# Attention stage of an attention-and-experts kernel: second buffers for K, Q and V as loaded, and an order of work taken from a written table of times

## The chip, the cores and the metric

The kernel runs on one core of one Trainium2 chip. The metric is the device time of one execution in microseconds (us). A core has five instruction streams that run side by side and wait for each other by semaphores: TensorE (PE, with its weight loads shown apart as PEld), VectorE (DVE), ScalarE (ACT), GpSimd (POOL) and SyncE (SP), which here issues nearly all DMA transfers of the attention stage. Each stream runs in the order in which the program was written.

## The reference

Attention over 8 batches and 8 heads with 1152 keys of 64 elements, the queries averaged in pairs (576 per head), and then a layer of 8 experts with a fixed capacity:

```python
def _attn_ref(q, k, v):
    B, H, S, D = q.shape                       # 8, 8, 1152, 64, float32
    scale = 1.0 / np.sqrt(D)
    q_pool = q.reshape(B, H, S // 2, 2, D).mean(axis=3)
    scores = scale * np.matmul(q_pool, k.transpose(0, 1, 3, 2))
    scores = scores - np.max(scores, axis=-1, keepdims=True)
    attn = np.exp(scores)
    attn = attn / (np.sum(attn, axis=-1, keepdims=True) + 1e-09)
    return np.matmul(attn, v).astype(np.float32)

def reference(...):
    x = attn_out.transpose(0, 2, 1, 3).reshape(B * S, H * D)   # 4608 x 512
    return _moe_ref(x=x, ...)   # logits x @ w_gate, capacity 576 per expert,
                                # relu(x @ w1[e]) @ w2[e], float32
```

## The kernel before

The work on attention runs over 32 pairs of heads, two heads side by side on the 128 partitions. A pair goes through these steps, named here by the tags of the code:

- Loads on SP: `lq` (queries, tile QD, 576 KB), `lk` (keys, tile KD, in two halves of 288 KB), `lv` (values, tile VD, 576 KB). There is one buffer of each.
- Preparation: `qs` on DVE adds the two queries of each average; `ka` and `qa` on ACT sum absolute values; `ks` (four tiny DVE steps) makes a scale; `qh`, `kh` on ACT and `ql`, `kl` on DVE split Q and K into a high and a low float16 part. `kl` is the last reader of KD. Copies on SP spread the parts over the operand tiles: `s1`, `s2`, `s3` for keys, `s4`, `s5`, `s6` for queries, `bd` for a block-diagonal query operand. `vabs`, `vs`, `vh`, `vl` do the same for V.
- Row maxima: `mm` on PE multiplies high parts into the PSUM tiles mt, `mr` on DVE reduces them (tile MX), `fold`, `augt`, `aug`, `augd` turn them into an extra row of the query operand.
- The main loop of 18 steps a pair: `qk` on PE (two matmuls, tile sc, three PSUM banks in turn), `exp` on ACT (tile P), `pm` on POOL or DVE (tile PM, the rounding rest of P), `av` on PE in groups of one or two steps; `rc` and `x` on DVE divide the result into tile X.
- Every second pair, `gt`, `gc`, `gm`, `gl` apply the gate weights to the finished columns and `store` writes X to DRAM.
- Constant tables for the experts stage (`routing_tables`), and at the start matmuls on constants (`wu`, `wv`) and `fill`s.

All of these are given to `Order.add` with a program position t, an engine, an assumed duration, the resources read and written, and a tag. `Order.emit` derives what must follow what, and then plays a list schedule: it keeps a clock per engine, takes whichever ready step can start first, breaks ties by t plus a hand-found lead per tag (`LEAD`), adds assumed latencies (`OWN`, `WAIT`, `LATE`), and keeps DVE and POOL steps marked `lock` from overlapping in its own clocks. The order in which this play starts the steps is the order in which the instructions are written to the engines. The experts stage has an `Order` of its own.

Of the kernel before, what the change touches and what calls it, by code (L numbers as in the profile page):

```python
# [1433 lines left out]
```

## Time and profile before

| | us |
|---|---|
| median of 3 runs | 1302.24 (1299.56 to 1303.64) |
| the profiled execution, its own time | 1307.96 |
| its span, first to last instruction | 1306.20 |
| PE, DVE, ACT, POOL busy in the span | 1247.8, 1038.2, 769.9, 777.7 |
| attention, first instruction to the last `av` | 802.4 |

Busy time is the union of an engine's instructions. PE's ends are modelled, so a busy PE is not a PE at its peak. The profiled execution took 5.7 us more than the median run; sums over the trace are made against 1307.96.

### The profile page before, as it was taken

The numbers are of one execution on the slowest core, as the hardware profiler recorded it, in microseconds if no ns is written. First come the engines' busy times: TensorE is split into PE (matmuls) and PEld (weight loads), VectorE is DVE, ScalarE is ACT, GpSimd is POOL, SyncE is SP. The second block draws the span as 40 slices with busy tenths as digits, with TensorE's granted clock in tenths as the row PEclk, the third lists the DMA queues.
The fourth block names the chain that finished last, engine by engine and source line by source line (L and its number), as shares of the span: only waits on it lengthen the run. The fifth ranks groups of instructions, "written<-read, shape, count | busy, mean of one in ns | idle before, by whom it ended". The sixth has DMA issues, their size and how long they took to land.

```text
span 1306.2 us, 39238 instructions
## 1 busy us (share of the span) xinstructions
PE 1247.8 (96%) x15419; PEld 1008.1 (77%) x15419; DVE 1038.2 (79%) x2606; ACT 769.9 (59%) x1901; POOL 777.7 (60%) x746
## 2 busy tenths in 40 slices
PE   7899999999999999999999997799999999999996
PEld 4577787777777777777777776587978889798895
DVE  8999999999999999899999985898876767752120
ACT  4588777877877877877877864143333324334330
POOL 5275576565656656656657563257667667586631
PEclk8799999999999999999999998999999999999998
DMA  4655555654654654654655520225445343454301
GB/s 150 154 167 144 156 151 139 174 148 126 186 145 121 178 147 117 177 150 119 181 149 140 126 60 20 66 102 197 170 133 150 130 126 124 151 172 143 125 14 37
DMA packets 123541, 175.25 MB, mean 134 GB/s; under 512 B 49500, under 2 KB 86364, under 8 KB 121180
## 3 DMA queue, kind: packets, MB, share of 16 engines
q1 hardware_dynamic: 114876, 120.29, 34.2%
q0 software_dynamic: 8336, 52.44, 11.5%
q8 instruction: 121, 1.98, 0.7%
q14 instruction: 64, 0.52, 0.1%
q10 hardware_dynamic: 144, 0.02, 0.0%
HBM read 99.63 MB, written 18.87 MB: 91 GB/s over the span
## 4 chain that ended last, share of the span: by engine, by line
PE 72%; DVE 16%; issue 5%; DMA 4%; ACT 1%; SPq 1%; POOL 0%; POOLq 0%; DVEq 0%; ACTq 0%
PE ph L1327 16%; PE av L617 14%; PE po L1357 13%; PE mt L497 8%; PE sc L600 8%; PE sc L601 7%; DVE MX L524 4%; DVE PM L607 4%; DMA KA<-KL 2%; DMA KD<-in_kt_dram 1%; PE mt L658 1%; PE po L1354 1%; DVE KL L442 1%; DMA QA<-QH 1%; PE rt L1001 1%
## 5 line engine op out<-in xcount | busy, mean ns | idle before, releaser
L607 POOL TENSOR_TENSOR PM<-P 128x576 f16<-128x576 f32 x413 | 473.4, 1174 | 312.4 <-ACT P L604 263.8
L604 ACT ACTIVATE P<-sc 128x288 f32<-128x288 f32 x1152 | 396.1, 413 | 162.7 <-PE sc L601 151.4
L524 DVE TENSOR_REDUCE MX<-mt 128x2 f32<-128x768 f32 (+1 forms) x443 | 399.4, 919 | 47.1 <-PE mt L497 43.8
L600 PE MATMUL sc<-QA,KA 128*128 128x288 f16 x1152 | 309.9, 286 | 10.9 <-ACT P L604 8.9
L617 PEld LDWEIGHTS <-P 128*128 128x128 bf16 x5760 | 297.5, 98 | 27.8 <-issue 0.7
L601 PE MATMUL sc<-QB,KB 66*128 66x288 f16 (+1 forms) x1152 | 311.7, 288 | 0.6 <-DMA QB<-AU 0.4
L617 PE MATMUL av<-V,P 128*128 128x65 f16 (+1 forms) x5760 | 306.0, 193 | 1.2 <-DVE V L483 1.2
L617 PE MATMUL av<-V,PM 128*128 128x65 f16 x2880 | 296.4, 195 | 0.0
L617 PEld LDWEIGHTS <-PM 128*128 128x128 f16 x2880 | 265.4, 97 | 1.3 <-issue 1.3
L497 PE MATMUL mt<-KH,BD 128*128 128x384 f16 x837 | 200.2, 326 | 3.4 <-DVE MX L524 1.6
L1357 PE MATMUL po<-W2H,HX 128*128 128x512 f32 x512 | 168.2, 399 | 0.0
L601 PEld LDWEIGHTS <-KB 66*128 66x128 f16 (+1 forms) x1152 | 112.0, 97 | 66.7 <-issue 29.6
L1327 PE MATMUL ph<-XH,W1H 128*128 128x320 f32 (+1 forms) x512 | 153.0, 299 | 1.0 <-issue 0.5
L1327 PE MATMUL ph<-XL,W1H 128*128 128x320 f32 (+1 forms) x512 | 152.4, 298 | 1.6 <-DVE XL L1226 1.5
L1327 PE MATMUL ph<-XH,W1L 128*128 128x320 f32 (+1 forms) x512 | 152.3, 298 | 1.0 <-issue 1.0
L600 PEld LDWEIGHTS <-KA 128*128 128x128 f16 x1152 | 112.9, 98 | 49.5 <-issue 15.7
L1332 ACT ACTIVATE HX<-ph 128x256 fp32r<-128x256 f32 (+1 forms) x128 | 51.5, 413 | 134.0 <-PE ph L1327 125.5
L607 DVE TENSOR_TENSOR PM<-P 128x576 f16<-128x576 f32 x163 | 123.5, 767 | 6.4 <-ACT P L604 5.5
L1357 PE MATMUL po<-W2L,HX 128*128 128x512 f32 (+1 forms) x320 | 127.6, 399 | 0.0
L1336 DVE SCALAR_TENSOR_TENSOR HX<-ph,HX 128x256 fp32r<-128x256 f32 x128 | 52.9, 415 | 81.1 <-ACT HX L1332 77.6
L1357 PEld LDWEIGHTS po<-W2H,HX 128*128 128x128 f32 x512 | 95.3, 189 | 18.5 <-issue 1.7
L497 PEld LDWEIGHTS <-BD 128*128 128x128 f16 x837 | 75.3, 98 | 30.8 <-issue 10.4
(233 smaller groups left out, 1899.7 us busy)
## 6 DMA issues: line engine op xcount, KB each, us to landing
QD<-in_qt_dram SPq DMA_DIRECT2D x32, 576.0 KB
KD<-in_kt_dram SPq DMA_DIRECT2D x64, 288.0 KB
VD<-in_v_dram SPq DMA_DIRECT2D x32, 576.0 KB
QA<-QH SPq DMA_DIRECT2D x128, 72.0 KB
KA<-KH SPq DMA_DIRECT2D x64, 144.0 KB
KB<-KH SPq DMA_DIRECT2D x64, 144.0 KB
KA<-KL SPq DMA_DIRECT2D x64, 144.0 KB
x_dram<-X SPq DMA_DIRECT2D x16, 576.0 KB
```

The source lines that it names most:

```text
L442: od.add(t + 5 + 2 * z, "DVE", 727, lock=1, fn=lambda h=h: nc.vector.scalar_tensor_tensor(KL[0][:, h], KD[0][:, h], sk, KH[i][:, h], op0=O ...
L497: nc.tensor.matmul(out, BD[i][:, j], KH[i][:, ks], start=True, stop=True)
L524: od.add(t, "DVE", d, lambda: nc.vector.tensor_reduce(dst, src, axis=AX.X, op=OP.max), r=[mk], w=[("MX", i, j, c) for j, c in what], tag=" ...
L600: nc.tensor.matmul(c[:, :288], KA[i][:, s, ks], QA[i][:, s, qs], start=True, stop=False)
L601: nc.tensor.matmul(c[:, :288], KB[i][:kr, s, ks], QB[i][:kr, s, qs], start=False, stop=True)
L604: od.add(g + 0.1 + 0.01 * t, "ACT", 293, lambda c=c, qs=qs: nc.scalar.activation(p[:, qs], c[:, :288], AF.Exp, scale=1.0 / UNIT), r=[ck], ...
L607: od.add(g + 0.2, en, dur, lock=1, fn=lambda: eng.tensor_tensor(pm, p, hi, op=OP.subtract), r=[("P32", g % NP, 0), ("P32", g % NP, 1)], w= ...
L617: nc.tensor.matmul(out, w[:, qs], v, start=kb == 0 and j == 0 and y == 0, stop=kb == NKB - 1 and y == 2, skip_group_check=True)
L1327: nc.tensor.matmul(p, a[:, d, fs], b[:, d, qs], start=z == 0, stop=z == 11)
L1332: nc.scalar.activation(HH[:, f, qs], p, AF.Relu)
L1336: V.scalar_tensor_tensor(HL[:, f, 64 + 256 * hf:320 + 256 * hf], p[:, :256], 0.0, h[:, :256], op0=OP.max, op1=OP.subtract)
L1357: nc.tensor.matmul(o[:n], a[:, z, q0:q0 + n], b[:, z], start=z == 0 and y == 0, stop=z == 7, skip_group_check=True)
```

## The change

Tiles KD, QD and VD get a second buffer (pair n uses buffer n % 2), so the load of pair n+1 no longer has to follow the last reader of pair n. The list schedule of the attention stage is replaced by `Timed`: each step has a name (its tag, its index k, and a letter that counts repeats within a pair), and an entry in a table of times in ns. The entry counts from the start of its pair, and pair n starts at n x 23600. Pairs 0 to 3 and the last two (`y`, `z`) have rows of their own; all others use the rows `e` (even) and `o` (odd), so the order repeats every two pairs. `emit` writes, among the steps whose predecessors have been written, the one with the smallest time. Clocks, latencies, leads and the `lock` marks play no part any more. Which engine does which step, durations, tiles other than the three, and the experts stage are unchanged.

```diff
-    od = Order(LEAD, LATE)
-    od.stick = AT["stick"]
+    od = Timed(TIME, PERIOD, npair)
...
-    KD = several(1, [128, S], F32, "KD")
-    QD = several(1, [128, 2, M], F32, "QD")
-    VD = several(1, [128, 2, NKB, D], F32, "VD")
+    KD = several(2, [128, S], F32, "KD")
+    QD = several(2, [128, 2, M], F32, "QD")
+    VD = several(2, [128, 2, NKB, D], F32, "VD")
...
-            od.add(t, "SP", 1200, lambda h=h: nc.sync.dma_start(KD[0][:, h], kt[n][:, h]), w=[("KD", z)],
+            od.add(t, "SP", 1200, lambda h=h: nc.sync.dma_start(KD[n % 2][:, h], kt[n][:, h]), w=[("KD", n % 2, z)],
                    late=2000, tag="lk", k=z)
...
+class Timed(Order):
...
+    def when(self, i):
+        n, name, t = self.names[i]
+        if name is None:
+            return -1e6
+        for p in ("0123" + "-" * self.pairs)[n] + ("yz"[n - self.pairs + 2] if n + 2 >= self.pairs else "-") + "eo"[n % 2]:
+            if p + name in self.table:
+                return n * self.period + self.table[p + name]
+        return t / NSTEP * self.period + self.period
+
+    def emit(self):
+        items = sorted(range(len(self.items)), key=lambda i: (self.items[i][0], i))
...
+        heap = [(self.when(items[i]), i) for i in range(n) if not left[i]]
+        heapq.heapify(heap)
+        done = 0
+        while heap:
+            _, i = heapq.heappop(heap)
+            self.items[items[i]][4]()
+            done += 1
+            for j in users[i]:
+                left[j] -= 1
+                if not left[j]:
+                    heapq.heappush(heap, (self.when(items[j]), j))
...
+PERIOD = 23600
...
+        "0filli": -28725, "0fillj": -12920, "0folda": -21352, "0foldb": -7681, "0foldc": -7038, "0foldd": 13293,
+        "0folde": -14699, "0foldf": -7378, "0foldg": -151, "0foldh": -12930, "0iqa": -16700, "0iqb": -12237,
+        "0iqc": -29805, "0iqd": -12930, "0kaa": -62092, "0kab": -2174, "0kh0a": -47325, "0kh1a": -47135,
...
+        "0kse": -10509, "0lk0a": -50752, "0lk1a": -38077, "0lqa": -47701, "0lva": -18899, "0mca": -11093,
...
+        "1ksa": -53738, "1ksb": -50821, "1ksc": -60593, "1ksd": -47555, "1lk0a": -62969, "1lk1a": -63095,
...
+        "2s41a": -19505, "2s50a": -20003, "2s51a": -31364, "2s60a": -34079, "2s61a": -28738, "2tablesa": -6078,
...
+        "2tablesg": -16860, "2tablesh": -12541, "2tablesi": -14357, "2tablesj": 701, "2tablesk": 7222,
...
+        "eaugdb": -29239, "eaugta": -5367, "eav0a10a": 20821, "eav0a12a": 24000, "eav0a14a": 22376,
+        "eav0a16a": 21085, "eav0a17a": 26168, "eav0a1a": 8204, "eav0a3a": 10245, "eav0a5a": 12272,
...
+        "eexpb8a": -6966, "eexpb9a": -3860, "efolda": -14291, "ekaa": -51818, "ekh0a": -38345, "ekh1a": -37948,
...
+        "elk0a": -61297, "elk1a": -62910, "elqa": -61161, "elva": -28886, "emm0a": -28007, "emm10a": -11157,
+        "emm11a": -10503, "emm12a": -7204, "emm13a": -7242, "emm1a": -28007, "emm2a": -28006, "emm3a": -28007,
...
+        "epm8a": -28584, "epm9a": -34115, "eqaa": -48418, "eqha": -47273, "eqka0a": 509, "eqka10a": 11977,
...
+        "eqkb6a": 7807, "eqkb7a": 7808, "eqkb8a": 8004, "eqkb9a": 12284, "eqla": -38350, "eqsa": -51227,
+        "erc0a": -9682, "erc1a": -14578, "erca": -15138, "ercb": -14666, "es10a": -16229, "es11a": -15107,
+        "es20a": -28887, "es21a": -28767, "es30a": -16422, "es31a": -16463, "es40a": -16508, "es41a": -16583,
+        "es50a": -16584, "es51a": -27951, "es60a": -31159, "es61a": -24359, "evabsa": -12829, "evh0a": -1161,
...
+        "oav0a8a": 17942, "obda": -39843, "obdb": -38791, "oexpa0a": 1968, "oexpa10a": -7384, "oexpa11a": -1477,
...
+        "ogcb": 2554, "ogla": -47730, "ogma": 39737, "ogpa": -45501, "ogta": 20686, "ogtb": 34983, "okaa": -55857,
...
+        "oksc": -60791, "oksd": -46190, "olk0a": -75548, "olk1a": -75143, "olqa": -72386, "olva": -37173,
...
+        "oqka0a": 2054, "oqka10a": 12901, "oqka11a": 13075, "oqka12a": 13711, "oqka13a": 16231, "oqka14a": 13651,
...
+        "os40a": -40304, "os41a": -39329, "os50a": -41912, "os51a": -35235, "os60a": -37173, "os61a": -29675,
...
-    for _ in range(AT["wu"]):
-        od.add(-70, "PE", 60, lambda: nc.tensor.matmul(mt[0][:, 0, :128], ones, ones, start=True, stop=True), w=["m0"])
+    for z in range(AT["wu"]):
+        od.add(-70, "PE", 60, lambda: nc.tensor.matmul(mt[0][:, 0, :128], ones, ones, start=True, stop=True), w=["m0"], tag="wu", k=z)
...
-    od.cur = None
+    od.cur, od.pair = None, 2
     C = routing_tables(nc, top, ident, jp, scratch,
-                       lambda eng, dur, fn: od.add(2 * NSTEP, eng, dur, fn, w=["tables"]))
+                       lambda eng, dur, fn: od.add(2 * NSTEP, eng, dur, fn, w=["tables"], tag="tables"))
```

The same renaming by n % 2 is made in every reader of the three tiles (`split`, `values`). In the table 1625 entries stand; those quoted are the ones that the prediction speaks of.

## Rows read from the trace of the kernel before

**Rows 1.** The page's first lines: the span, and each engine's busy us (share of the span) x instructions.

```profile
span 1306.2 us, 39238 instructions
...
PE 1247.8 (96%) x15419; PEld 1008.1 (77%) x15419; DVE 1038.2 (79%) x2606; ACT 769.9 (59%) x1901; POOL 777.7 (60%) x746
```

**Rows 2.** Busy time of each engine in stretches of the attention stage. The columns are the stretch and its length, busy us (and instructions) of PE, PEld, DVE, ACT and POOL, PE's granted clock, the mean busy share of the DMA engines, and GB/s. Each stretch but the last runs from one maximum reduction to the same one two pairs later, as the chain that ended last shows them (the one that ends at 582.82 holds four pairs). Twelve such two-pair stretches lie between 149.33 and 725.11. The last row is the start, up to pair 1's first matmul on sc.

```profile
149.33:196.50 47.17, 47.05 (x763) 37.06 (x760) 44.71 (x84) 37.57 (x96) 29.55 (x27) 1.00 0.57 154
196.50:243.67 47.17, 47.05 (x763) 37.02 (x760) 44.71 (x84) 37.60 (x96) 29.54 (x27) 1.00 0.56 153
243.67:291.97 48.30, 47.26 (x766) 37.24 (x763) 44.85 (x86) 37.62 (x96) 29.67 (x27) 1.00 0.54 146
...
435.64:484.69 49.05, 47.26 (x766) 37.24 (x763) 44.85 (x86) 37.62 (x96) 29.71 (x27) 1.00 0.54 147
484.69:582.82 98.13, 94.45 (x1520) 73.97 (x1517) 89.82 (x167) 75.35 (x192) 59.29 (x53) 1.00 0.55 147
...
677.80:725.11 47.31, 47.14 (x763) 37.02 (x760) 44.73 (x85) 37.62 (x96) 29.47 (x27) 1.00 0.57 153
0.00:64.18 64.18, 49.75 (x527) 34.71 (x528) 56.51 (x131) 33.51 (x76) 26.66 (x41) 0.79 0.54 152
```

**Rows 3.** Who waited for whom in 243.67 to 582.82 us: us in total, times, longest us.

```profile
ACT VJ L406 <- DMA KD<-in_kt_dram: 8.1, 7, 1.8
PE sc L600 <- ACT P L604: 6.2, 7, 1.1
...
PE sc L600 <- DMA VD<-in_v_dram: 1.7, 1, 1.7
```

**Rows 4.** One place of such a wait, 446 to 457 us, in order of time: start, length, engine, line, operation, tiles; in brackets the idle time before it and what ended it. K's release on DVE, the issues on SP, ACT, and PE.

```profile
446.86 1.54 DVE L442 SCALAR_TENSOR_TENSOR KL<-KD,KS,KH 128x576 f16<-128x576 f32 x2
...
449.21 1.73 SPq L392 DMA_DIRECT2D KD<-in_kt_dram  x2
...
450.96 2.15 ACT L604 ACTIVATE P<-sc 128x288 f32<-128x288 f32 x6 [0.16 <-PE sc L601]
454.88 1.16 ACT L406 ACTIVATE VJ<-KD 128x1152 bf16<-128x1152 f32 x1 [1.77 <-DMA KD<-in_kt_dram]
...
456.48 0.28 PE L600 MATMUL sc<-QA,KA 128*128 128x288 f16 x1 [1.68 <-DMA VD<-in_v_dram]
```

**Rows 5.** Loads and copies on SP: duration in ns (min/median/max) of the issuing instructions on SP, first and last start; then the GB/s of 100 to 300 us in 40 slices.

```profile
L392 SPq DMA_DIRECT2D KD<-in_kt_dram x64: 333/522/1456, 1.2 to 722.7; - x64
...
L389 SPq DMA_DIRECT2D QD<-in_qt_dram x32: 328/530/2188, 0.8 to 713.3; - x32
...
L450 SPq DMA_DIRECT2D QA<-QH x128: 463/595/2037, 10.7 to 760.2; - x128
...
L450 SPq DMA_DIRECT2D KA<-KH x64: 482/595/1982, 12.0 to 759.6; - x64
...
GB/s 252 142 84 236 132 77 36 178 279 145 162 172 119 210 121 26 113 257 148 249 148 97 250 109 62 64 170 261 191 209 81 107 221 121 21 113 186 222 208 168
```

**Rows 6.** The start on DVE and SP, in order of time (columns as in rows 4).

```profile
0.76 0.40 SPq L389 DMA_DIRECT2D QD<-in_qt_dram  x1
1.21 0.91 SPq L392 DMA_DIRECT2D KD<-in_kt_dram  x2
2.17 0.43 SPq L396 DMA_DIRECT2D VD<-in_v_dram  x1
...
1.58 0.64 DVE L384 MEMSET P<- 128x64 f32 x10
...
2.55 3.54 DVE L373 TENSOR_SCALAR ndiag<-scratch 128x576 f32<-128x576 int32 x2
6.01 0.74 DVE L401 TENSOR_TENSOR QS<-QD 128x576 f32<-128x576 f32 x1
...
23.54 0.22 DVE L267 TENSOR_SCALAR before<-jp 128x128 bf16<-128x128 int32 x1
...
26.54 1.80 DVE L276 TENSOR_SCALAR nib<-scratch 128x16 f32<-128x16 int32 x2
...
28.99 1.14 DVE L281 TENSOR_SCALAR diag<-scratch 128x64 f16<-128x64 int32 x1
30.16 1.10 DVE L282 TENSOR_TENSOR diag<-diag,scratch 128x64 f16<-128x64 f16 x1
...
31.58 0.95 DVE L524 TENSOR_REDUCE MX<-mt 128x2 f32<-128x768 f32 x1
...
32.57 0.48 DVE L288 CAST slots<-scratch 128x640 f16<-128x640 int32 x1
```

**Rows 7.** Line 607, the step `pm`: its instructions on POOL and on DVE, duration in ns (min/median/max).

```profile
L607 POOL TENSOR_TENSOR PM<-P x413: 1140/1147/1713, 25.0 to 797.9; 128x576 f16<-128x576 f32 x138
...
L607 DVE TENSOR_TENSOR PM<-P x163: 736/748/1689, 35.6 to 798.9; 128x576 f16<-128x576 f32 x163
```

**Rows 8.** The first matmul on sc of pairs 6, 7 and 8, in order of time (columns as in rows 4).

```profile
182.22 0.28 PE L600 MATMUL sc<-QA,KA 128*128 128x288 f16 x1
...
208.24 0.28 PE L600 MATMUL sc<-QA,KA 128*128 128x288 f16 x1
...
229.39 0.28 PE L600 MATMUL sc<-QA,KA 128*128 128x288 f16 x1
```

More of the change, by code (lines that the diff above doesn't have):

```diff
@@ L1 @@
+import heapq
 import math
@@ L158, in emit, with __init__, add @@
             items[i][4]()
+class Timed(Order):
+    def __init__(self, table, period, pairs):
+        Order.__init__(self)
+        self.table, self.period, self.pairs = table, period, pairs
+        self.pair, self.names, self.seen = 0, [], {}
+    def add(self, t, eng, dur, fn, r=(), w=(), late=0, first=0, tag=None, kind=0, lock=None, k=None):
+        Order.add(self, t, eng, dur, fn, r, w, late, first, tag, kind, lock)
+        name = ("pm" if tag in ("pmP", "pmD") else tag or "o") + ("" if k is None else str(k))
+        z = self.seen[self.pair, name] = self.seen.get((self.pair, name), -1) + 1
+        self.names.append((self.pair, name + "abcdefghijklmnopqrstuvwxyz"[z] if z < 26 else None, t))
+    def when(self, i):
[8 more added lines that the diff above has]
+        items = sorted(range(len(self.items)), key=lambda i: (self.items[i][0], i))
+        writer, readers, n = {}, {}, len(items)
+        need = [set() for _ in range(n)]
+        for i, j in enumerate(items):
+            _, _, _, _, _, r, w, _, _ = self.items[j]
+            for k in r:
+                if k in writer:
+                    need[i].add(writer[k])
+                readers.setdefault(k, []).append(i)
+            for k in w:
+                if k in writer:
+                    need[i].add(writer[k])
+                need[i].update(readers.get(k, ()))
+                readers[k] = []
+                writer[k] = i
+            need[i].discard(i)
+        users, left = [[] for _ in range(n)], [len(x) for x in need]
+        for i, x in enumerate(need):
+            for j in x:
+                users[j].append(i)
+        heap = [(self.when(items[i]), i) for i in range(n) if not left[i]]
[9 more added lines that the diff above has]
+                    heapq.heappush(heap, (self.when(items[j]), j))
+        assert done == n
@@ L300, in attention @@
     psum = ctx.enter_context(tc.tile_pool(name="att_psum", bufs=1, space=PSUM))
-    od = Order(LEAD, LATE)
-    od.stick = AT["stick"]
-    od.early = ("qs", "qh", "bd", "kh", "kl", "ql", "mm", "mc", "mr", "fold", "aug", "augt")
+    od = Timed(TIME, PERIOD, npair)
     jp = const.tile([128, 128], I32, name="jp")
@@ L388, in load @@
     def load(n, t):
-        od.add(t, "SP", 2440, lambda: nc.sync.dma_start(QD[0], qt[n]), w=["QD"], late=2000, tag="lq")
+        od.add(t, "SP", 2440, lambda: nc.sync.dma_start(QD[n % 2], qt[n]), w=[("QD", n % 2)], late=2000, tag="lq")
         for z in range(2):
             h = slice(z * M, z * M + M)
-            od.add(t, "SP", 1200, lambda h=h: nc.sync.dma_start(KD[0][:, h], kt[n][:, h]), w=[("KD", z)],
+            od.add(t, "SP", 1200, lambda h=h: nc.sync.dma_start(KD[n % 2][:, h], kt[n][:, h]), w=[("KD", n % 2, z)],
                    late=2000, tag="lk", k=z)
     def load_v(n, t):
-        od.add(t, "SP", 2500, lambda: nc.sync.dma_start(VD[0], v[n]), w=["VD"], late=2500, tag="lv")
+        od.add(t, "SP", 2500, lambda: nc.sync.dma_start(VD[n % 2], v[n]), w=[("VD", n % 2)], late=2500, tag="lv")
     def split(n, t):
         i = n % 2
-        od.add(t, "DVE", 666, lock=1, fn=lambda: nc.vector.tensor_tensor(QS[0], QD[0][:, 0], QD[0][:, 1], op=OP.add),
-               r=["QD"], w=["QS"], tag="qs")
+        od.add(t, "DVE", 666, lock=1, fn=lambda: nc.vector.tensor_tensor(QS[0], QD[n % 2][:, 0], QD[n % 2][:, 1], op=OP.add),
+               r=[("QD", n % 2)], w=["QS"], tag="qs")
         if n:
-            od.add(t + .5, "ACT", 1150, lambda: nc.scalar.activation(VJ, KD[0], AF.Abs, accum_out=KS[i][:, 0:1]),
-                   r=[("KD", 0), ("KD", 1)], w=[("KN", i)], tag="ka")
+            od.add(t + .5, "ACT", 1150, lambda: nc.scalar.activation(VJ, KD[n % 2], AF.Abs, accum_out=KS[i][:, 0:1]),
+                   r=[("KD", n % 2, 0), ("KD", n % 2, 1)], w=[("KN", i)], tag="ka")
         else:
@@ L439, in split @@
             h = slice(z * M, z * M + M)
-            od.add(t + 4 + 2 * z, "ACT", 670, lambda h=h: nc.scalar.activation(KH[i][:, h], KD[0][:, h], AF.Copy, scale=sk),
-                   r=[("KD", z), ("SK", i)], w=[("KH", i, z)], tag="kh", k=z)
+            od.add(t + 4 + 2 * z, "ACT", 670, lambda h=h: nc.scalar.activation(KH[i][:, h], KD[n % 2][:, h], AF.Copy, scale=sk),
+                   r=[("KD", n % 2, z), ("SK", i)], w=[("KH", i, z)], tag="kh", k=z)
             od.add(t + 5 + 2 * z, "DVE", 727, lock=1, fn=lambda h=h: nc.vector.scalar_tensor_tensor(
-                KL[0][:, h], KD[0][:, h], sk, KH[i][:, h], op0=OP.mult, op1=OP.subtract),
-                r=[("KD", z), ("SK", i), ("KH", i, z)], w=[("KL", z)], tag="kl", k=z)
+                KL[0][:, h], KD[n % 2][:, h], sk, KH[i][:, h], op0=OP.mult, op1=OP.subtract),
+                r=[("KD", n % 2, z), ("SK", i), ("KH", i, z)], w=[("KL", z)], tag="kl", k=z)
     def spread(n, t):
@@ L726, in attention @@
     od.cur = None
-    for _ in range(AT["wu"]):
-        od.add(-70, "PE", 60, lambda: nc.tensor.matmul(mt[0][:, 0, :128], ones, ones, start=True, stop=True), w=["m0"])
-    for _ in range(AT["wv"]):
+    for z in range(AT["wu"]):
+        od.add(-70, "PE", 60, lambda: nc.tensor.matmul(mt[0][:, 0, :128], ones, ones, start=True, stop=True), w=["m0"], tag="wu", k=z)
+    for z in range(AT["wv"]):
         od.add(-42, "PE", 54, lambda: nc.tensor.matmul(av[:, :128], ones, ones, start=True, stop=True),
-               r=[("CM", 0, 0)], w=["av"], first=-1)
+               r=[("CM", 0, 0)], w=["av"], tag="wv", k=z)
     for i in range(2):
@@ L736, in attention @@
         base = NSTEP * (n - 1)
-        od.cur = n
+        od.cur = od.pair = n
         if n == 0:
@@ L776, in attention @@
     for g in range(npair * NSTEP):
-        od.cur = g // NSTEP
+        od.cur = od.pair = g // NSTEP
         step(g)
     for n in range(1, npair, 2):
-        od.cur = None
+        od.cur, od.pair = None, n
         g = NSTEP * n + NSTEP
@@ L793, in attention @@
         store(n, g + LAG + 1)
-    od.cur = None
+    od.cur, od.pair = None, 2
     C = routing_tables(nc, top, ident, jp, scratch,
-                       lambda eng, dur, fn: od.add(2 * NSTEP, eng, dur, fn, w=["tables"]))
+                       lambda eng, dur, fn: od.add(2 * NSTEP, eng, dur, fn, w=["tables"], tag="tables"))
     od.emit()
```

30 lines of the change are left out of this document (20 added, 10 removed), and 307 rows, old and new, of tables (LATE, LEAD, TIME).

## The prediction

> **What bounds the kernel now.** I read four things in this order: the engines' shares, the busy time in equal pieces of the attention stage, the list of waits in the worse pieces, and one such wait instruction by instruction. The shares say that PE is busy for 96% of the span [rows 1], so time can only come from PE's few idle places or from work that leaves PE's queue, and the change takes no work away. The reader should then look at the pieces of two pairs each [rows 2]. The program repeats there, and the best pieces take 47.17 us, with PE busy for 47.05 and DVE for 44.71. Two engines are nearly full: DVE has 47.17 - 44.71 = 2.46 us left in two pairs. Other pieces hold the same work (763 or 766 matmuls, 96 ACT instructions) and take 48.30, 49.05, and 98.13 for four pairs, while PE's busy time grows by only 0.2 in a two-pair piece. The difference is idle PE.
>
> The waits name it [rows 3]: in 243.67 to 582.82 us PE waits for ACT's `exp` 7 times, 6.2 us, and once more 1.7 us under the name of a V load; ACT waits for the K load 7 times, 8.1 us. One of them in detail [rows 4]: `kl`, the last reader of the only K buffer, ends at 448.40. SP issues both K halves between 449.21 and 450.94. ACT has finished its `exp`s by 453.11 and comes to `ka`, which needs K: it stands until 454.88, some 4.3 us after the second issue began. The `exp`s behind `ka` are late by as much, the three score banks are full, and PE sits 1.68 us before its next `qk`. The V load in that row is only the event nearest in time; the `qk` waits for a bank. So a K buffer that is freed late, a load of about 4 us and a place on ACT's queue too close to it cost about 1 us in more than half of the middle periods.
>
> **The change, part by part.**
>
> *Second buffers and earlier loads.* The table puts the K load of an even pair 62.9 and 61.3 us ahead of its pair and `ka` at 51.8, thus about 10 us between them; for an odd pair 75.5 and 55.9, about 20. Before, it was 4.3. The release by `kl` no longer matters, since the other buffer's last reader lies a pair back. What it is worth: twelve periods lie between 149.33 and 725.11, which is 575.78 us; twelve undisturbed ones are 12 x 47.17 = 566.04 [rows 2]. That is 9.7 us. I take all of it, because every stall in these pieces has the same shape. Bounds: 0, if `ka` is still late, and 9.7.
>
> *The repeated order.* Its bounds are wide. If every hidden wait went, a period could fall to DVE's 44.71, 13 x 2.46 = 32 us less over pairs 4 to 29; if it hits as badly as the worst piece, 49.05, it loses 13 x 1.88 = 24. I take 0, for the table looks like the undisturbed periods of this trace: an even and the following odd pair start at 182.22 and 208.24, the next even one at 229.39, 26.02 and 21.15 us apart [rows 8], and the table's first `qk` of an even and an odd pair are 23.6 + 2.05 - 0.51 = 25.1 apart, then 22.1. Work per engine is the same. At the places where PE needs DVE at once (`augt` after `fold`, `gt` after a maximum) I find in the table about the distance the trace has.
>
> *SP's queue.* To find a step's place I take the later of its own entry and those of the steps that it must follow. Around 31 us after an even pair's start this bunches transfers: seven operand copies of the next even pair (0.79 MB), four of the next odd one (0.29), then between them the K halves and Q of the pair four ahead (1.15). That is 14 issues, 11 x 0.595 + 3 x 0.525 = 8.1 us by the medians of rows 5, so Q is issued near 30.6 + 8.1 = 38.7 and read by `qs` on DVE at 94.4 - 51.2 = 43.2. Behind it on SP wait only copies needed 10 us and more later. The 2.2 MB take 8.0 us at the best slice's 279 GB/s [rows 5] and 14.6 at the 153 of a mean period [rows 2]: 38.6, or 45.2. I take no cost, since a bunch issued in one go is nearest to a full slice, and keep up to 3 us of DVE wait a period as the upper end (45.2 plus the landing, against 43.2).
>
> The Trainium skill (DMA: Bandwidth & Descriptors, Anatomy of one DMA) gives a transfer about 2.0 us plus its bytes over 436 GB/s, estimated 2.7 us for a K half; rows 4 show 4.3 from issue to use, so the measurement is the slower one. By the page's figures Q would land near 42.1 and nobody would wait, and the sum would be the same as mine.
>
> *The start.* The constant tables leave it: DVE spends 26.54 to 31.58 mostly on them, 5.0 us, and two shorter bits at 23.54 and 32.57 [rows 6]; they go to pairs 2 and 3, where DVE's 2.46 us of slack a period takes half. Against that, the memsets and the two `ndiag` steps, done from 1.58 to 6.09 while DVE waited for Q, get entries at -12.9 and -12.2, among the work ahead of the first `qk`: 1.0 us and up to 3.5. And pair 1's K halves (576 KB) stand on SP ahead of pair 0's second K half (-39.5 against -38.1): 2.1 to 3.8 us by the two rates above, in a start whose first loads were issued from 0.76 on and read from 6.01 on. DVE has 64.18 - 56.51 = 7.7 us idle in the start [rows 2] to soak up some. Bounds: 5 us better to 8 worse; I take 0, as the two sides are of one size. Pairs 30 and 31 and the experts stage: 0, same work.
>
> *Sum.* 1307.96 - 9.7 = 1298.3 for the profiled execution. The median run is 5.7 us faster than that; carried over, 1292.5. Part of the 5.7 may be milder stalls, and then less is to be had, at the least 9.7 - 5.7 = 4. I say **1293**, and 1287 to 1300 for this case alone.
>
> **Rivals.**
>
> *The period shrinks too.* For it: some 2.5 us a period are idle on DVE, and the table moves many steps by a microsecond or two. Against it: two engines at 95% and more, chained through two maximum banks and three score banks. Half of the floor's gain is 16 us: 1277.
>
> *Given back.* `ka` is on time, but another step in the fixed order now stands about 0.7 us a period, for example the even pair's `augt`, placed 1.8 us after the last `mm`, which DVE must first reduce (0.95 each [rows 6]). 13 x 0.75 = 9.7, hence no change: 1302. That the buffers alone do nothing, because `ka` still waits, ends at the same time; 10 us against 4.3 speaks against it.
>
> *Slower: the burst.* If SP's bunch moves at 153 GB/s, Q comes up to 3.5 us late and DVE stands in `qs`, with the reductions behind it. It decides from 2.46 us of wait on, DVE's slack; at 3.5 it is 13 x 1.0 us over the forecast, 1306, and with the start's 5 worse 1311. Against it: five of the forty slices move 250 GB/s or more [rows 5], so the engines can do it when there is work queued.
>
> *Slower: DVE and POOL collide.* The list schedule kept `lock` steps apart in its clocks; the table doesn't know them. A `pm` takes 736 to 1689 ns on DVE and 1140 to 1713 on POOL [rows 7], and tiny table steps stretch to 1.1 us [rows 6]: one collision is about 0.95. Slack covers 2.6 a period; five of the ten DVE `pm`s hit would cost 4.75 - 2.46 = 2.3, so 30 us: 1323. Against it: the order is close to that of before, where the medians are at the minima. The Trainium skill (SBUF — State Buffer, Who interferes with whom) has the pair of ports as an exclusive lock that goes to whoever issues first; the longest rows agree with it.
>
> **Chances.** Forecast 0.53, shorter period 0.11, given back or no effect 0.18, burst 0.12, collisions 0.06. What this measurement can tell from no change is 0.3%, 3.9 us: under 1298.3 counts as faster, over 1306.1 as slower. From the forecast 0.03 falls within: faster 0.61, same 0.21, slower 0.18. The range 1276 to 1309 leaves out the far end of the shorter period, the collisions and the worse half of the burst.
>
> **What would show it.** In the profile after: ACT's wait for the K load gone or under 1 us in all after 150 us; even pieces of 47.2 us throughout, with the same busy times; PE's waits for `exp` near zero there; SP issuing an even pair's K loads about 10 us or more before `ka`. Wrong would be: DVE waiting for the Q load, pieces that all have the same new length other than 47.2, longer `pm` rows, or pair 1 starting more than 5 us away from 64.18.

## The result, and the profile after

The changed kernel is slower: 1310.64 us against 1302.24 in the median, a ratio of 1.0051 (95% interval 1.0030 to 1.0071), where 1293 and "faster" had been predicted. Measured a second time, on another chip, the ratio was 1.0055 (1.0034 to 1.0077). The page of the changed kernel's profiled execution, which took 1306.12 us (4.5 us less than its median run), begins:

```profile
span 1304.3 us, 39111 instructions
...
PE 1239.5 (95%) x15419; PEld 1004.5 (77%) x15419; DVE 1053.9 (81%) x2606; ACT 784.8 (60%) x1901; POOL 783.1 (60%) x746
```

The two spans say nothing here: the profiled execution of before [rows 1] was a long one among its runs, that of after a short one. The stages can be compared. The columns are as in [rows 2]; the cuts are the first matmuls on sc of pairs 1, 2, 3, 4 and 28 and the last `av`; the last row is the experts stage. Before:

```profile
0.00:64.18 64.18, 49.75 (x527) 34.71 (x528) 56.51 (x131) 33.51 (x76) 26.66 (x41) 0.79 0.54 152
64.18:87.46 23.28, 21.65 (x328) 16.51 (x326) 22.30 (x43) 19.26 (x49) 15.73 (x13) 1.00 0.52 143
87.46:113.48 26.02, 25.92 (x424) 20.27 (x421) 24.97 (x50) 21.87 (x54) 14.79 (x13) 1.00 0.65 182
113.48:135.04 21.56, 21.20 (x345) 16.75 (x342) 19.72 (x36) 15.76 (x42) 14.76 (x13) 1.00 0.44 114
135.04:710.82 575.78, 566.13 (x9099) 444.97 (x9096) 537.58 (x1001) 451.34 (x1152) 355.53 (x312) 1.00 0.55 150
710.82:802.38 91.56, 91.37 (x1539) 73.00 (x1536) 74.30 (x133) 65.29 (x173) 59.06 (x55) 1.00 0.32 85
802.38:1306.19 503.81, 471.83 (x3189) 401.92 (x3185) 302.83 (x1220) 162.92 (x355) 291.14 (x299) 0.97 0.37 120
```

After:

```profile
0.00:65.89 65.89, 45.91 (x513) 31.94 (x513) 52.53 (x114) 37.46 (x82) 23.85 (x30) 0.84 0.55 153
65.89:90.44 24.55, 23.78 (x370) 18.54 (x369) 22.32 (x39) 17.80 (x46) 18.50 (x24) 0.95 0.60 151
90.44:120.28 29.84, 25.80 (x390) 19.31 (x388) 27.42 (x69) 21.67 (x52) 15.11 (x13) 1.00 0.41 116
120.28:142.50 22.22, 21.56 (x342) 16.93 (x340) 21.64 (x37) 16.93 (x45) 15.48 (x13) 1.00 0.60 161
142.50:714.35 571.85, 562.01 (x9094) 444.36 (x9093) 549.68 (x1000) 460.39 (x1152) 360.95 (x312) 1.00 0.57 152
714.35:806.06 91.71, 90.48 (x1532) 72.52 (x1529) 77.25 (x131) 65.92 (x171) 58.20 (x55) 1.00 0.30 77
806.06:1304.32 498.26, 469.95 (x3195) 400.86 (x3191) 303.07 (x1221) 164.65 (x355) 291.03 (x299) 0.98 0.37 122
```

Row by row, after minus before: +1.71, +1.27, +3.82, +0.66 (7.46 lost by pair 4), -3.93 in the twelve two-pair periods of pairs 4 to 27, +0.15 in pairs 28 to 31. Attention is 3.68 us longer. The experts stage, the same code, was 5.55 us shorter in this execution; in the second profile of the changed kernel, the run after_again, it took 504.96 us, and attention 806.99. So a gain is there, and the first four pairs lose nearly twice as much. The forecast for attention comes to 802.38 - 9.74 = 792.64 us; of the 13.42 by which it was missed, 7.46 are lost by pair 4, 5.81 in the twelve periods and 0.15 in the last pairs.

The gain first. ACT's wait for K, the first row of [rows 3], is gone. The place that answers to [rows 4], in order of time: SP issues both K halves at 427.60, and `ka` reads them at 445.01, 17.4 us later, without waiting.

```profile
427.60 1.34 SPq L662 DMA_DIRECT2D KD<-in_kt_dram  x2
...
445.01 1.18 ACT L676 ACTIVATE VJ<-KD 128x1152 bf16<-128x1152 f32 x1
```

The best two-pair periods now take 47.45 us, not 47.17 [rows 2], and ten of the twelve are within 0.2 us of that. One of the best (columns as above):

```profile
190.09:237.54 47.45, 46.76 (x758) 36.99 (x757) 45.73 (x84) 38.35 (x96) 30.08 (x26) 1.00 0.56 152
```

PE is idle for 0.69 us of it, against 0.12 before. Two short waits stand in every period, `mm` for a maximum bank and the one-column matmul on V's maxima for ACT's `vabs`; their sums over 135 to 758 us (us, times, longest) and one example of each:

```profile
PE mt L767 <- DVE MX L794: 5.8, 13, 0.5
...
PE mt L739 <- ACT VJ L736: 2.9, 13, 0.2
```

```profile
586.81 0.16 PE L739 MATMUL mt<-VM,ones 128*128 128x1 bf16 x1 [0.22 <-ACT VJ L736]
...
593.89 0.27 PE L840 MATMUL mt<-ident,CM 128*9 128x128 f32 x1
...
594.59 0.65 PE L767 MATMUL mt<-KH,BD 128*128 128x384 f16 x3 [0.42 <-DVE MX L794]
```

The loss is clearest in pair 2 (29.84 against 26.02 us). The larger block of constant tables, 98.39 to 102.20 us, stands there in one piece on DVE; a reduction waits behind it, and PE 1.08 us for that:

```profile
97.53 0.95 DVE L794 TENSOR_REDUCE MX<-mt 128x2 f32<-128x768 f32 x1
98.39 1.62 DVE L548 TENSOR_SCALAR nib<-scratch 128x16 f32<-128x16 int32 x2
...
101.99 0.21 DVE L564 CAST TAB<-scratch 128x1 f16<-128x1 int32 x2
...
102.36 0.95 DVE L794 TENSOR_REDUCE MX<-mt 128x2 f32<-128x768 f32 x1
```

```profile
103.36 0.48 PE L767 MATMUL mt<-KH,BD 128*128 128x384 f16 x2 [1.08 <-DVE MX L794]
```

The waits of PE in pair 2, from 90.44 to 120.28 us, make up nearly all of the 3.8 us (before, pair 2 had none over 0.15):

```profile
PE sc L870 <- ACT P L874: 1.8, 5, 0.7
...
PE mt L767 <- DVE MX L794: 1.3, 2, 1.1
...
PE mt L942 <- DVE VE L743: 0.4, 1, 0.4
...
PE av L887 <- DVE X L909: 0.2, 1, 0.2
```

So the largest part is PE waiting five times for an `exp` to free a score bank. Pair 1's 1.27 us are mostly the clock. From 60.0 to 64.9 us PE was busy for only 2.04 us; from 64.9 to 68.3 it was then granted the lower of its two levels (1.2 and 2.4 GHz). In the kernel before, pair 1 ran at the upper one throughout. At the rate of the rest of the pair, 349 matmuls in 21.37 us, the 23 that fall into pair 1 at the lower level would take 1.4 us and not 2.4, an estimate of 1.0 us lost:

```profile
60.00:64.90 4.90, 2.04 (x16) 0.85 (x13) 4.67 (x15) 2.15 (x5) 0.00 (x0) 1.00 0.07 16
...
65.89:68.30 2.41, 2.41 (x23) 1.85 (x22) 2.26 (x4) 2.08 (x5) 0.67 (x1) 0.50 0.27 61
...
68.30:90.44 22.14, 21.37 (x349) 16.69 (x347) 20.06 (x35) 15.72 (x41) 17.84 (x24) 1.00 0.63 161
```

At the very start the first `qk` comes at 33.90 us, not 23.70, but pair 1 only 1.7 us later than before.

### The profile page after: what moved, and what is told of

It is laid out like the page before. It is cut to its first block, busy times and chain, and to the rows that moved or that the text cites. A ratio compares the mean times of both kernels' runs of the same rounds, so it can differ in the third digit from the quotient of the medians.

```text
span 1304.3 us, 39111 instructions
## 1 busy us (share of the span) xinstructions
PE 1239.5 (95%) x15419; PEld 1004.5 (77%) x15419; DVE 1053.9 (81%) x2606; ACT 784.8 (60%) x1901; POOL 783.1 (60%) x746
## 4 chain that ended last, share of the span: by engine, by line
PE 72%; DVE 16%; issue 5%; DMA 3%; SPq 1%; ACT 1%; POOL 1%; DVEq 0%; POOLq 0%; ACTq 0%
PE ph L1597 16%; PE av L887 14%; PE po L1627 13%; PE mt L767 9%; PE sc L870 8%; PE sc L871 8%; DVE MX L794 5%; DVE PM L877 3%; DMA KA<-KL 2%; DVE KL L712 2%; PE po L1624 1%; PE mt L928 1%; SPq L720 1%; PE rt L1271 1%; DVE QS L671 1%
## 5 line engine op out<-in xcount | busy, mean ns | idle before, releaser
L877 POOL TENSOR_TENSOR PM<-P 128x576 f16<-128x576 f32 x413 | 479.2, 1185 | 310.0 <-ACT P L874 297.9
L874 ACT ACTIVATE P<-sc 128x288 f32<-128x288 f32 x1152 | 403.5, 412 | 136.0 <-PE sc L871 120.8
L794 DVE TENSOR_REDUCE MX<-mt 128x2 f32<-128x768 f32 (+1 forms) x443 | 392.9, 923 | 22.8 <-PE mt L767 16.3
L887 PEld LDWEIGHTS <-P 128*128 128x128 bf16 x5760 | 288.6, 98 | 22.9 <-issue 2.3
L887 PE MATMUL av<-V,P 128*128 128x65 f16 (+1 forms) x5760 | 296.5, 192 | 1.5 <-issue 1.3
L887 PE MATMUL av<-V,PM 128*128 128x65 f16 x2880 | 289.2, 195 | 0.1
L1606 DVE SCALAR_TENSOR_TENSOR HX<-ph,HX 128x256 fp32r<-128x256 f32 x128 | 53.6, 420 | 77.4 <-ACT HX L1602 77.2
L1627 PEld LDWEIGHTS po<-W2H,HX 128*128 128x128 f32 x512 | 95.4, 189 | 16.8
```

What stands on the lines that cost most here:

```text
L794: od.add(t, "DVE", d, lambda: nc.vector.tensor_reduce(dst, src, axis=AX.X, op=OP.max), r=[mk], w=[("MX", i, j, c) for j, c in what], tag=" ...
L874: od.add(g + 0.1 + 0.01 * t, "ACT", 293, lambda c=c, qs=qs: nc.scalar.activation(p[:, qs], c[:, :288], AF.Exp, scale=1.0 / UNIT), r=[ck], ...
L877: od.add(g + 0.2, en, dur, lock=1, fn=lambda: eng.tensor_tensor(pm, p, hi, op=OP.subtract), r=[("P32", g % NP, 0), ("P32", g % NP, 1)], w= ...
L887: nc.tensor.matmul(out, w[:, qs], v, start=kb == 0 and j == 0 and y == 0, stop=kb == NKB - 1 and y == 2, skip_group_check=True)
L1606: V.scalar_tensor_tensor(HL[:, f, 64 + 256 * hf:320 + 256 * hf], p[:, :256], 0.0, h[:, :256], op0=OP.max, op1=OP.subtract)
L1627: nc.tensor.matmul(o[:n], a[:, z, q0:q0 + n], b[:, z], start=z == 0 and y == 0, stop=z == 7, skip_group_check=True)
```

## The experiments

Every ratio is to the kernel before, run on the same chip in the same sitting, with its 95% interval. Several kernels use the old list schedule as a clock: `Timed` also plays it, with one buffer of each as before, writes nothing from it, and keeps each step's start, shifted so that pair 4's first `qk` falls on its time in the table.

**The change once more**, unaltered:

> The changed kernel as it is, beside the other runs of this chip, for its profile and its ratio to the kernel before here. If the ratio of 1.005 is the two orders' doing, it comes again between 1.003 and 1.008, with pair 4 at 142 to 143 us and even pieces of 47.5 us. Attention up to the last av should again be some 4 us longer than in the kernel before (806.1 against 802.4), and what is left of the ratio stands in the experts stage, whose code is the same.

Measured: 1.0055, as given above; pair 4 starts at 144.2 us, and pair 2 took 30.6.

**One part alone.** Second buffers, and every engine's instructions in the order of before:

```diff
-    KD = several(1, [128, S], F32, "KD")
+    KD = several(2, [128, S], F32, "KD")
...
-            od.add(t, "SP", 1200, lambda h=h: nc.sync.dma_start(KD[0][:, h], kt[n][:, h]), w=[("KD", z)],
+            od.add(t, "SP", 1200, lambda h=h: nc.sync.dma_start(KD[n % 2][:, h], kt[n][:, h]), w=[("KD", z)],
```

> The kernel before with a second buffer for K, Q and V; its planner still plans with one, so every engine's instructions stand in the same order as before. If the freeing of the K buffer by kl was what made K late, the waits of ACT for the K load go, the two-pair pieces fall to 47.2 us and the time drops by 5 to 10 us against the kernel before. If the place of the load on SP's queue was what made it late (in the profile of before SP waits for a reader of K, Q or V some 13 us in all over 576 us, at most 1.6 us at a time), the load is issued at most 1 to 1.5 us sooner, a part of ACT's waits stays, and the time falls by 0 to 3 us.

Measured: 1.0016 (0.9993 to 1.0039), no difference. ACT still waits for K 7 times, 6.5 us. The sum, and one place on DVE, SP and ACT: `kl` ends at 447.87, SP issues `bd` until 448.32, comes to the load at 448.37, and the load is late though it no longer has to wait for that `kl`.

```profile
ACT VJ L406 <- DMA KD<-in_kt_dram: 6.5, 7, 1.9
```

```profile
446.33 1.54 DVE L442 SCALAR_TENSOR_TENSOR KL<-KD,KS,KH 128x576 f16<-128x576 f32 x2
...
446.98 1.34 SPq L436 DMA_DIRECT2D BD<-QH  x2
448.37 1.81 SPq L392 DMA_DIRECT2D KD<-in_kt_dram  x2
...
454.51 1.16 ACT L406 ACTIVATE VJ<-KD 128x1152 bf16<-128x1152 f32 x1 [1.93 <-DMA KD<-in_kt_dram]
```

So the freeing of the buffer was not what made K late: SP only reached the load then. The place of [rows 4] itself shows it already, in the kernel before: SP issued `bd` until 449.10, 0.7 us after `kl` had ended.

```profile
447.77 1.33 SPq L436 DMA_DIRECT2D BD<-QH  x2
```

The Trainium skill (Trainium Kernel Development and Optimization, Best Practices) says to double-buffer so that transfers overlap computation; a second buffer alone changed nothing that can be measured here.

The reverse part, the table's order with one buffer:

```diff
-    KD = several(2, [128, S], F32, "KD")
+    KD = several(1, [128, S], F32, "KD")
```

> The changed kernel with one buffer each for K, Q and V, so that loads stand behind the last reader of the pair before and the table sets all else. In the table's own times that reader (kl, 73.7 us ahead of an odd pair) stands only 2 us behind the load (75.5) and ka 18 us behind it, so if the order of work and not the second buffer sets when K is there, the steady pieces stay at 47.5 us and the time within 2 us of the changed kernel, apart from its start, where pair 1's K now has to wait for pair 0's kl. If the second buffer is what took the K stalls away, they come back: pieces of 48 to 49 us and 5 to 10 us more than the changed kernel.

Measured: 1.0265 (1.0245 to 1.0286), by the ratios some 27 us slower than the changed kernel. The twelve periods take 590.84 us, not 571.85. There SP itself now stands before nearly every pair's K load until `kl` is through (24 times), and ACT waits for K again (first SP's waits, then ACT's):

```profile
SPq L662 <- DVE KL L712: 68.6, 24, 5.0
```

```profile
ACT VJ L676 <- DMA KD<-in_kt_dram: 17.4, 13, 2.4
```

My sum over the table's times, in which one buffer would hardly have mattered, was wrong: 2 us between entries are not 2 us between events.

**SP's order alone.** The order of before on PE, DVE, ACT and POOL, second buffers, and only loads moved ahead in SP's order (pairs 3 to 31):

```diff
+        early = 10000 if self.names[i][0] > 2 and self.names[i][1] in ("lk0a", "lk1a") else 0
+        return self.clock[i] - self.shift - early if True else self.table_time(i)
```

> The order of the kernel before on every engine and its second buffers, but the two K loads of pairs 3 to 31 stand 10 us earlier (by the planner's clock) in the order of SP. If K's place on SP's queue is what makes ka late, ACT's waits for K go, the two-pair pieces fall from 48 to 47.2 to 47.5 us, and the time drops 6 to 10 us below the kernel before. If those stalls were given back elsewhere anyway (work that PE waits for in any case), the pieces stay near 48 and the time within 3 us of the kernel before.

Measured: 0.9945 (0.9925 to 0.9966), 6.0 us between the medians. With 5000 in place of 10000:

> The same with K's loads 5 us earlier instead of 10, V as before. K stood 4.3 us ahead of ka and was 1.0 to 1.8 us late; 5 us more should cover that as well as 10: 6 to 7 us below the kernel before, as with 10, if lateness is all that counts; 2 to 4 us below if the distance matters beyond it.

Measured: 0.9963 (0.9941 to 0.9984), 4.8 us. ACT's waits for K are gone in both; with K 10 us ahead ACT waits for V instead (3.3 us, 4 times), with 5 us PE waits for the small copies `augd` (4.3 us, 8 times). The two intervals overlap. V as well, `{"lk": 10000, "lv": 3000}`:

> The order of the kernel before on PE, DVE, ACT and POOL, second buffers, K's loads 10 us earlier in SP's order and V's 3 us (pairs 3 to 31). If ACT's wait for V (3.3 us in four places of the run with K alone) is the rest of the prediction's 9.7 us: pieces of 47.2 to 47.4 us and 8 to 10 us below the kernel before. If an earlier V pushes the copies behind it on SP past their readers: no better than K alone, 6 to 7 us below, or worse.

Measured: 0.9919 (0.9891 to 0.9946), 10.4 us. The twelve periods:

```profile
134.71:704.45 569.74, 566.22 (x9100) 445.44 (x9096) 538.76 (x1001) 450.96 (x1152) 356.33 (x312) 1.00 0.56 152
```

The same kernel once more, on another chip:

> The kernel with two buffers, K 10 us and V 3 us early in the order of before, once more, beside the run with one buffer: 8 to 11 us below the kernel before, as in the first measurement (10.4), if that was no chance of one chip.

Measured: 0.9911 (0.9895 to 0.9928), 11.2 us, and

```profile
133.44:701.36 567.92, 565.88 (x9099) 445.38 (x9096) 537.46 (x1001) 450.60 (x1152) 355.79 (x312) 1.00 0.56 152
```

Before, the twelve periods took 575.78, and the prediction's undisturbed ones make 566.04: in these profiles 6.0 and 7.9 of the 9.7 us are won. This version beats both kernels.

Q 10 us and V 8 us ahead too:

```diff
+        early = 0 if self.names[i][0] < 3 else {"lk": 10000, "lq": 10000, "lv": 8000}.get((self.names[i][1] or "")[:2], 0)
```

> The run with K's loads 10 us earlier in the order of before, now with Q's loads 10 us and V's 8 us earlier as well (pairs 3 to 31). In that run ACT still waited for V four times, 3.3 us, and the pieces were 47.2 to 48.3 us. If those are the last of it, the pieces become 47.2 to 47.5 us and the time falls another 1 to 4 us, to 8 to 11 us below the kernel before. If the earlier bunch of loads only delays the operand copies behind them on SP, the pieces grow and the gain of 6 us is partly lost.

Measured: 1.0099 (1.0076 to 1.0122), slower. PE now waits for the copies of the maxima's row (`augd`, 1.1 KB each): 21.0 us, 14 times, up to 3.0. The sum from 130 to 780 us, and one of them, SP and then PE:

```profile
PE sc L1017 <- DMA QB<-AU: 21.0, 14, 3.0
```

```profile
252.62 0.58 SPq L812 DMA_DIRECT2D VD<-in_v_dram  x1
253.31 1.57 SPq L991 DMA_DIRECT2D QB<-AU  x2
```

```profile
258.68 0.30 PE L1017 MATMUL sc<-QB,KB 66*128 66x288 f16 x1 [2.71 <-DMA QB<-AU]
```

A V load of 576 KB is issued just ahead of the small copies; PE has the row 5.4 us after their issue began. In 13 of the 14 waits a V load is what SP issued last before these copies. The Trainium skill (DMA: Bandwidth & Descriptors, Queues, rings and completion order) states that each transfer engine consumes its ring's descriptors in order; the late copies fit that, though the trace has no landing times to show it.

The last cell, K and V early with one buffer (tiles and resources of KD, QD, VD as before):

> The order of the kernel before, K's loads asked for 10 us and V's 3 us earlier in SP's order, but one buffer each, so that a load can be written no sooner than behind the last reader of the pair before. If the second buffers are what makes room for the early load: SP now stands in front of kl with the operand copies behind it, ACT waits for K as before or more, and the time is at or above the kernel before (0 to 20 us slower; with the table's order one buffer cost 30 us). If the place on SP alone counts: within 3 us of the run with two buffers, thus 6 to 11 us below the kernel before.

Measured: 1.0070 (1.0046 to 1.0095), beside 0.9911 with two. The twelve periods take 585.08 us, and ACT waits for K 9 times, 10.6 us:

```profile
ACT VJ L818 <- DMA KD<-in_kt_dram: 10.6, 9, 2.6
```

Neither part works alone: the early order without the buffer is 0.7% slower, the buffer without the order nothing, both together 0.8 to 0.9% faster.

**The start.** First both orders joined at pair 4:

```diff
+    def when(self, i):
+        return self.clock[i] - self.shift if self.names[i][0] < 4 else self.table_time(i)
```

> Second buffers; pairs 0 to 3, the warm-up and the constant tables in the order of the kernel before (its own clocks, played with one buffer), pairs 4 to 31 in the order of the table. If the start is what the changed kernel loses (7.4 us up to the first qk of pair 4 in the two profiles), that goes, and the steady part keeps its gain of 5.3 us: 1 to 5 us below the kernel before, 6 to 10 below the changed one. If the steady order of the table is the loss, it is as slow as the changed kernel or within 2 us of it.

Measured: 1.0080 (1.0058 to 1.0102). Pair 1 starts at 62.4 us, but pair 2 takes 31.4, and pair 4 starts at 142.1. The mirror image:

> The mirror image: second buffers; pairs 0 to 3, warm-up and constant tables in the order of the table, pairs 4 to 31 in the order of the kernel before. If the start is the loss: 7 us above the run with the second buffers alone, pair 4 starts near 142 instead of 135 us. If the steady order is the loss: within 2 us of that run.

Measured: 1.0184 (1.0164 to 1.0203); pair 2 takes 37.1 us. Joined at pair 2 instead:

> As the run that joins the order of before to the table, but joined at pair 2: pairs 0 and 1, the warm-up and the constant tables in the order of before, pairs 2 to 31 by the table. If the seam at pair 4 cost the earlier run its 7 us (its pair 2 took 31.4 us), this one starts pair 4 at 134 to 138 us and comes 3 to 8 us below the changed kernel; if the table's rows of pairs 2 to 5 are themselves slow, pair 4 starts at 140 to 143 again.

Measured: 1.0140 (1.0115 to 1.0165), pair 1 at 77.2 and pair 4 at 157.6 us. A joint costs more than the start does; I take it that this is so because every pair's preparation stands among the steps of the two pairs ahead of it. These three settle nothing about the start alone.

Then the table's own entries. By the rule of the prediction (a step's place is the later of its own entry and those of the steps that it must follow) `0kab` at -2174 holds back pair 0's scale and `0foldd` at 13293 its first `qk`, behind steps of pairs 1 to 3. All entries of the matmuls on constants, `wu` and `wv`, go to -60000 with them:

```diff
-"0lk1a": -38077 ... "0kab": -2174 ... "0kse": -10509 ... "0foldd": 13293 ... "0foldg": -151
+"0lk1a": -47000 ... "0kab": -46000 ... "0kse": -46000 ... "0foldd": -7000 ... "0foldg": -7000
...
-"0wu0a": -12943 ... "0wv0a": -11818 ...
+"0wu0a": -60000 ... "0wv0a": -60000 ...
```

> The changed kernel with five entries of pair 0 moved: 0lk1a, 0kab, 0kse from -38077, -2174, -10509 to -47000, -46000, -46000, and 0foldd, 0foldg from 13293, -151 to -7000 (the warm-up matmuls, too, to -60000, so that they stay ahead). In the table 0kab holds back the whole of pair 0's preparation and 0foldd its first qk, so that everything of pairs 1 to 3 due before 13.3 us is written ahead of it. If these late entries are the start's loss: first qk 4 to 8 us sooner than 33.9 us, pair 4 at 135 to 139 us and the time 3 to 7 us below the changed kernel. If the loss is in pairs 1 and 2, which now have to take what stood ahead: pair 4 again at 141 to 144.

Measured: 1.0257 (1.0231 to 1.0282), much slower:

```profile
0.00:95.40 95.40, 61.76 (x513) 40.33 (x514) 52.78 (x114) 38.35 (x82) 22.97 (x30) 0.65 0.38 105
95.40:121.00 25.60, 24.82 (x371) 19.02 (x370) 22.28 (x39) 17.99 (x46) 18.54 (x24) 0.91 0.58 145
```

First `qk` at 42.8, pair 1 only at 95.4 us, and PE idle for 33.6 of those, not 20.0: now, as I read it, pair 1's preparation comes behind pair 0's. That is about half of the 29.5 us that pair 1 is later. The other half goes with PE's clock: the same 513 matmuls kept it busy for 61.8 us and not 45.9, at a granted 0.65 and not 0.84. This run moved the matmuls on constants, too, so it does not tell the order from them. The late first `qk` was in any case no loss of its size: the changed kernel has pair 1 ready 1.7 us after the kernel before. Two other repairs ended alike. Scale, memsets and `ndiag` of pair 0 early:

```diff
-"0lk1a": -38077 ... "0kab": -2174 ... "0kse": -10509 ... "0fillj": -12920 ... "0iqa": -16700 ...
+"0lk1a": -50000 ... "0kab": -50000 ... "0kse": -50000 ... "0fillj": -70000 ... "0iqa": -70000 ...
```

> The changed kernel with eight entries of pair 0 in the table moved: its second K half, the absolute sum over it and the last step of its scale go ahead of pair 1's work (0lk1a, 0kab, 0kse to -50000), the memsets and the ndiag steps ahead of everything (0fillj, 0iqa to 0iqd to -70000). If the late scale of pair 0 is what the start loses: first qk near 26 instead of 33.9 us, pair 4 starts 3 to 7 us sooner than 142.5, and the time falls by 3 to 7 us against the changed kernel. If the loss up to pair 4 arises in pair 2, where the constant tables stand on DVE: first qk earlier, but pair 4 within 2 us of 142.5.

Measured: 1.0128 (1.0104 to 1.0151), first `qk` at 42.3 us, pair 4 at 150.9. And pair 0's Q load and copies early, too, with `0foldd`, `0foldg`, `wu` and `wv` as above and pair 1's preparation late:

```diff
-"0lqa": -47701 ... "0s40a": -6361 ... "0s10a": -2771 ... "1kaa": -61760 ... "1qsa": -54153 ... "1kl1a": -47122 ...
+"0lqa": -52000 ... "0s40a": -24000 ... "0s10a": -24000 ... "1kaa": -35000 ... "1qsa": -37600 ... "1kl1a": -27100 ...
```

> The same with more of pair 0 put right: its operand copies, its Q load, memsets and ndiag steps early, and pair 1's preparation (ka, qa, qs, ks, kh, qh, kl) 10 to 25 us later, behind pair 0's maxima. First qk near 24 to 27 us, as before. If pair 0's own chain was held up by pair 1's work, pair 4 comes at 134 to 138 us and the time drops 4 to 8 us below the changed kernel; if pairs 1 and 2 need what was done early, pair 1 or 2 is late by as much and pair 4 stays at 141 or more.

Measured: 1.0285 (1.0262 to 1.0308), first `qk` at 34.6, pair 1 at 97.0, pair 4 at 175.6 us.

The constant tables moved, in the end ahead of pair 0's loop, since `0foldd` holds that back:

```diff
-"2tablesa": -6078    ...  "2tablesj": 701      "2tablesk": 7222     "2tablesl": 967
+"2tablesa": -56200   ...  "2tablesj": -56200   "2tablesk": -55000   "2tablesl": -51000
```

> The changed kernel with the twelve steps of the constant tables moved from pair 2 into pair 0's main loop (entries 2tablesa to 2tablesl at -56200 to -51000), where the kernel before has them. If their 4.5 us on a nearly full DVE are what makes pair 2 take 29.9 instead of 26.0 us: pair 3 comes 26 us after pair 2 and pair 4 starts 3 to 4 us sooner than 142.5, or, if DVE is as full in pair 0, the same loss shows there and pair 4 stays within 1.5 us of 142.5.

Measured: 1.0062 (1.0042 to 1.0083). First `qk` 4.1 us later than in the changed kernel, and pair 2:

```profile
96.00:124.60 28.60, 25.65 (x390) 19.31 (x388) 23.68 (x47) 22.02 (x54) 15.12 (x13) 1.00 0.42 121
```

The tables cost pair 2 about 1.2 us (29.84 to 28.60), the wait shown above. The other 2.6 of its 3.8 us are not theirs: PE's wait for a maximum is down to 0.2 us, the others stand as they were.

```profile
PE sc L870 <- ACT P L874: 1.8, 5, 0.7
...
PE mt L767 <- DVE MX L794: 0.2, 1, 0.2
```

Last, pairs 2 and 3 by the even and odd rows instead of their own:

```diff
-            if p + name in self.table:
+            if p + name in self.table and (p not in "23" or name[:6] == "tables"):
```

> The changed kernel with pairs 2 and 3 ordered by the even and odd rows of the table instead of rows of their own (the constant tables keep theirs). If those rows are what makes pair 2 take 29.9 us and pairs 0 to 3 7 us longer than before: pair 2 takes 26.4 to 27.5 us, pair 4 starts at 138 to 141 instead of 142.5 to 144, and the time falls 2 to 5 us below the changed kernel. If the cause is that pairs 0 and 1 leave too little done: pair 2 still takes 29 us or more.

Measured: 1.0208 (1.0182 to 1.0233); pair 2 takes 42.2 us and pair 4 starts at 165.5. The same with the constant tables in pair 0's loop:

```diff
-"2tablesa": -6078    ...  "2tablesj": 701      "2tablesk": 7222     "2tablesl": 967
+"2tablesa": -36000   ...  "2tablesj": -32000   "2tablesk": -29000   "2tablesl": -26000
```

> The same, and the constant tables moved from pair 2 into the later half of pair 0's loop, behind its first qk (the entries 2tablesa to 2tablesl to -36000 to -26000). If their 4.5 us on DVE cost 1 to 2 us in pair 2 (that much fell away there when they were moved ahead of the first qk, which cost 4 at the first qk), pair 4 starts 1 to 2 us sooner than in the run with the even and odd rows alone; if DVE is as full in pair 0, no sooner.

Measured: 1.0192 (1.0166 to 1.0219), pair 4 at 161.6 us. The rows that pairs 2 and 3 have of their own are better than the even and odd ones there, whatever they cost; taking the constant tables out of pair 2 again gave 3.9 us by pair 4.

## Why the prediction was wrong

*Second buffers and earlier loads, -9.7.* The mechanism (a late load holds up `ka`, the `exp`s behind it, the score banks, PE) was right, and its size nearly: K and, with it, V put ahead in the old order gave 10.4 and 11.2 us in the medians, and the profiles show 6.0 and 7.9 in the twelve periods. Two things were wrong. I put half the blame on the buffer's last reader; the buffer alone gave nothing, and in the very place of [rows 4] SP came to the load only 0.7 us after `kl` had ended. And I took all 9.7 for the changed kernel, where the twelve periods won 3.9.

*The repeated order, 0.* This step failed by 3 to 4: 12 x (47.45 - 47.17) = 3.4 us, and two periods of 48.0 and 48.5 make up most of the rest of the 5.8 that lack. The two waits of 0.45 and 0.22 us a period are of the kind I said I had looked for, PE needing DVE or ACT at once; I read the distances as "about" those of the trace, and half a microsecond was what counted. They add up to 0.67 us a period. PE's idle time rose by 0.57 and its busy time, whose ends are modelled, fell by 0.29, which leaves the 0.28 lost; no run takes the two waits away by themselves. It is the rival *given back*, at 0.3 us a period, not at 0.75.

*SP's queue, 0.* Right: after pair 4 DVE never waits for a Q load. The fit quoted there from the Trainium skill (DMA: Bandwidth & Descriptors, Anatomy of one DMA) is given for transfers that GpSimd issues; these loads are SP's, and no run here shows that fit for them. That a bunch can do harm was also right, but not where I looked for it: when Q and V were moved ahead, it was the 1.1 KB copies behind a big load that came late.

*The start, 0 with bounds of -5 to +8.* This is the step that turned the sign: +7.46, at the far end of its bounds. I priced what moved ahead of the first `qk` and called the tables' stay in pairs 2 and 3 half free, 2.5 us; for the new order of pairs 1 to 3 I had no term. The first `qk` came 10 us later and cost 1.7; pair 1 lost 1.3, about 1.0 of it at the lower clock; pair 2 lost 3.8, of which the tables are 1.2 and PE's five waits for `exp` 1.8; pair 3 lost 0.7. The waits are shown; which entries of pair 2's rows cause them stays open, for no run moved those one by one.

*Pairs 30 and 31, 0.* Right, with 28 and 29 taken in: +0.15 (some work moved from these into the last two).

*From the profiled execution to the median, -5.7.* Nothing on the path measured it, and for the changed kernel it had the other sign: its profiled execution was 4.5 us below its median. The experts stage of the same code took from 498.26 to 510.61 us over the profiles of this study; a sum of stages should be held against stages.

*The other rivals.* Collisions of DVE and POOL: refuted for `pm`, whose medians are those of [rows 7]; over 149 to 724 us, after:

```profile
L877 POOL TENSOR_TENSOR PM<-P x316: 1138/1146/1767, 149.1 to 724.0; 128x576 f16<-128x576 f32 x158
...
L877 DVE TENSOR_TENSOR PM<-P x120: 743/750/760, 155.8 to 714.0; 128x576 f16<-128x576 f32 x120
```

A period shorter than 47.17 us appeared in no run between pairs 4 and 28.

Of what I named as signs: ACT's K wait gone, right; K loads about 10 us or more ahead, right (8 to 18 us from the second issue); no DVE wait for Q, right; even pieces of 47.2, wrong, with one new length as the sign of error said; pair 1 within 5 us of 64.18, true, and yet no proof of a good start, which pair 4 would have been.

## What to carry to other kernels

A second buffer only permits an earlier load; it is the load's place in the order of the queue that issues it that uses the permission, so try the two as a table of four (here 1.002, 1.007 and 0.992 beside 1). Move the load whose wait the profile shows, and look at what then stands behind it in the queue: small copies pay (PE waited for them 4.3 us with K 5 us ahead, 0.5 with 10, and 21.0 with Q and V ahead as well). For a new order, sum the stages separately, the first pairs with their own term, and hold them against the stages of the other profile.

## What the runs showed of the hardware

A copy of 1.1 KB issued 0.7 us behind a load of 576 KB reached its reader 5.4 us after its issue began. The same 513 matmuls of the start kept PE busy for 45.9 us at a granted clock of 0.84 and for 61.8 at 0.65. The experts stage, the same instructions each time, varied by 12 us between executions and chips, more than the whole change.
